# Layer norm applies ahead of the last k norm, tile 1's statistics on ScalarE, and a split V matmul pair at the start

## The chip, the cores and the metric

The kernel runs on one core of a Trainium2 chip. The metric is device time in microseconds (us), the median of several executions. All ratios below are the mean time of one kernel's fast runs over the mean time of the other's fast runs in the same rounds on the same chip, so they are not quite the ratio of the medians quoted beside them. The profile is of one execution, and its span, first to last instruction, is about 1.7 us shorter than the device time.

## The reference, cut to what matters

```python
xn = layernorm(x)                        # x: 2048 x 448, 16 tiles of 128 rows
q, k, v = split_heads(xn @ wqkv)         # 16 heads of 28
phi(t) = concat(softmax(t @ w_phi), softmax(-(t @ w_phi)))
attn = (phi(q) @ sum(phi(k)^T v)) / (phi(q) . sum(phi(k)) + 1e-6) @ wo
h    = gelu(layernorm(xn) @ w1)          # four quarters, shifted by 1, -1, 2, -2 rows
x1   = xn + shifted(h) @ w2
out  = x + attn + x1 + gelu(layernorm(x1) @ w3) @ w4
```

The first layer norm stands at the start of everything. The layer norm of `x1` ("LN2") needs `w2`'s output; the softmax of k ("k norm") is needed by the matmuls that sum `phi(k)^T v` ("kv").

## The kernel before

Every operation is recorded with what it reads and writes, and the waits between engines follow from that. The order on each engine is the order of recording. TensorE works mostly in pairs of 64-row matmuls, one on the lower and one on the upper half of its rows, and a product comes in two halves: in the second each row half goes to the other's output bank.

```python
def lap_pair(outs, lhs, rhs):
    ...
    return (lambda: row_pairs(side(0, LO, (0, 1, 2, 3)), side(1, HI, (0, 1, 2, 3)), True),
            lambda: row_pairs(side(1, LO, (0, 1, 3)), side(0, HI, (0, 2, 3))))

def ln1_two(i):                     # first layer norm, tiles 0..3
    for j in (i, i + 1):
        ln_stats(st, mv, xtok, j)                              # VectorE
        R.act(rs[:, j, 1:2], mv[:, j, 1:2], ACT.Sqrt, bias=epsb[:, 0:1])   # ScalarE
    for j in (i, i + 1):
        R.ew(dve, "reciprocal", rs[:, j, 0:1], rs[:, j, 1:2])
        ln1_apply(dve, j)

ln1_two(0)
spin(19, 256)                       # filler matmuls
play([(xn_T, 0, 0), (spin, 3, 256), (xn_T, 1, 1)])             # transposes and eviction
ln1_two(2)
...
play([(spin, 4, 256), V(0, 0), (xn_T, 2, 0), V(0, 1), (xn_T, 3, 1),
      (spin, 2, 256), V(2, 0), (v_out, 0, 2), (tables, "gelu_apprx_tanh_and_others"),
      WA(0, 0), (xn_T, 4, 1), V(2, 1), ...

def k_norm(i):
    ph = phik[:, i:i + 2, :, 0:DH].rearrange("p t g e -> p (t g) e")
    ...
    R.ew(dve, "tensor_reduce", k, ph, axis=AX.X, op=ALU.add)
    R.ew(dve, "reciprocal", rk, k)
    R.ew(pool, "tensor_tensor", ph, ph, rk..., op=ALU.mult)    # GpSimd, 3.2 us
...
play([(g_apply, 4, dve), (g_apply, 5, dve), G(4, 5), (ln_scale, mv2, rs2, 6, 2, 0),
      (g_apply, 6, dve), (g_apply, 7, dve), G(6, 7),
      a(0), (wl[11][0],), b(0), a(1), K(10, 11), b(1), K(12), a(2), K(13), b(2), a(3), K(14, 15), ...
```

`g_apply` is the apply of LN2, `G` the DMA that transposes its result into `gT`, `a` and `b` the two halves of a `w3` pair that reads `gT`, `K` the kv matmuls, `WA` the first matmuls of the gelu branch.

The softmax here doesn't subtract the row's maximum and nothing guards it: scores larger than these inputs give would overflow.

Of the kernel before, what the change touches and what calls it, by code (L numbers as in the profile page):

```python
# [5 lines left out]
ACT = mybir.ActivationFunctionType  # L6
ALU = mybir.AluOpType
AX = mybir.AxisListType
BF16 = mybir.dt.bfloat16
F32 = mybir.dt.float32  # L10

LN_EPS = 1e-5
# [208 lines left out]
def bass_parallel_sum__linear_kernel_hedgehog__mixer_s_mlp__prompt_kernel(  # L221
    nc, A_x, A_wqkv, A_w_phi, A_wo, B_x, B_w1, B_w2, B_w3, B_w4, out,
):
    _, S, D = A_x.shape
    H, DH = A_w_phi.shape[0], A_w_phi.shape[1]
# [10 lines left out]
    with es:  # L236
        R = Recorder(nc, es)
# [13 lines left out]
        def new(name, cols, dt=BF16):  # L251
            return view(region(name, cols * DTB[dt]), cols, dt)
# [6 lines left out]
        banks = [pairs[b // 2][:, 512 * (b % 2):512 * (b % 2) + 512] for b in range(8)]  # L259


        xtok = new("xtok", NT * D).rearrange("p (t d) -> p t d", t=NT)
        xn = new("xn", NT * 512).rearrange("p (t d) -> p t d", t=NT)
        xnT_r = region("xnT", KC * S * 2)
        xnT = view(xnT_r, KC * S).rearrange("p (c s) -> p c s", c=KC)
# [38 lines left out]
        ksum = new("ksum", 4 * 32, F32).rearrange("p (b c) -> p b c", b=4)  # L304
        rks = new("rks", 4 * 32, F32).rearrange("p (b c) -> p b c", b=4)
        mhalf = new("mhalf", 8, F32)
        epsb = new("epsb", 8, F32)

        h3T = view(phik_r, 2 * FC * 512).rearrange("p (b c f) -> p b c f", b=2, c=FC)
        oT = view(xnT_r, 2 * KC * 512).rearrange("p (b c s) -> p b c s", b=2, c=KC)  # L310
# [74 lines left out]
        def tables(name):  # L385
            R.op("ACT", lambda e: e.preload_act_table_set(name), [], [])

        tables("sqrt_and_others")
        R.ew(pool, "memset", ident[:, :], 0.0)
        R.op(pool, lambda e: e.affine_select(ident[:, :], ident[:, :], pattern=[[-1, 128]],  # L390
                                             compare_op=ALU.not_equal, fill=1.0, base=0, channel_multiplier=1),
# [4 lines left out]
        R.ew(pool, "memset", hD[:, :, 512:DW], 0.0)  # L396
        busy = gT[:, 0, 0, 0:256]
        R.ew(dve, "memset", busy, 1.0)
        R.ew(dve, "memset", epsb[:, :], LN_EPS)
        R.ew(dve, "memset", vp[:, :, DH + 1:HP], 0.0)  # L400
        R.ew(dve, "memset", vp[:, :, DH:DH + 1], 1.0)
        mb = maskb[0:CR, :].rearrange("p (h e) -> p h e", h=4)
# [33 lines left out]
        def ln_stats(stt, mvt, src, i):  # L436
            R.ew(dve, "bn_stats", stt[:, i, 0:6], src[:, i, 0:D])
            R.ew(dve, "bn_aggr", mvt[:, i, 0:2], stt[:, i, 0:6])
# [17 lines left out]
        def ln1_apply(eng, i):  # L456
            ln_apply(eng, halves(xn[:, i, :]), lap(xtok[:, i, :]), mv, rs, i)
# [3 lines left out]
        def spin(n, cols):  # L461
            for _ in range(n):
                R.mm(banks[7][:, 0:cols], busy[:, 0:128], busy[:, 0:cols], True, True)
# [51 lines left out]
        def row_pairs(first, second, start=False, cols=1):  # L515
            for s, (p, q) in enumerate(zip(first, second)):
                for out, lhs, rhs in (p, q) if cols == 1 else (*p, *q):
                    R.mm(out, lhs, rhs, start and s == 0, False)

        def lap_pair(outs, lhs, rhs):  # L520
            def side(k, rows, kcs):
                return [(outs[k], lhs(k, kc, *rows), rhs(k, kc, *rows)) for kc in kcs]
            return (lambda: row_pairs(side(0, LO, (0, 1, 2, 3)), side(1, HI, (0, 1, 2, 3)), True),
                    lambda: row_pairs(side(1, LO, (0, 1, 3)), side(0, HI, (0, 2, 3))))
# [9 lines left out]
                            lambda k, kc, lo, hi: xnT[lo:hi, kc, 512 * g:512 * g + 512])  # L534

        def v_pair(i, b):
            return lap_pair([banks[2 * b + k][:, 0:D] for k in range(2)],
                            lambda k, kc, lo, hi: xnT[lo:hi, kc, 128 * (i + k):128 * (i + k) + 128],
                            lambda k, kc, lo, hi: wv[lo:hi, kc, :])

        def v_out(i, b, eng="ACT"):
            vd = vaug[:, i:i + 2, :].rearrange("p t (h e) -> p t h e", e=HP)[:, :, :, 0:DH]
# [80 lines left out]
            e = (eq_lo if g < 2 else eq_hi)[:, c:c + 2, s, 512 * (g % 2):512 * (g % 2) + 512]  # L623
            R.act(e, two(2 * b), ACT.Exp, scale=1.0 - 2.0 * s)

        def k_norm(i):
            ph = phik[:, i:i + 2, :, 0:DH].rearrange("p t g e -> p (t g) e")
            r = 2 * (i // 2 % 2)
            k, rk = (t[:, r:r + 2, :].rearrange("p b c -> p (b c)") for t in (ksum, rks))
            R.ew(dve, "tensor_reduce", k, ph, axis=AX.X, op=ALU.add)  # L630
            R.ew(dve, "reciprocal", rk, k)
            R.ew(pool, "tensor_tensor", ph, ph, rk.unsqueeze(2).to_broadcast([128, 4 * H, DH]), op=ALU.mult)

        def kv_tile(i):
            def side(k, rows):
# [32 lines left out]
        def g_apply(i, eng="POOL"):  # L668
            ln_apply(eng, halves(g_tok[:, i % 4, :]), lap(xn[:, i, :]), mv2, rs2, i)

        def g_T(i):
            j = 128 * (i % 4)
            R.dma_t(gT[:, (i // 4) % 2, :, j:j + 128], g_tok[:, i % 4, :])
# [106 lines left out]
        def play(fs):  # L780
            for f in fs:
                f[0](*f[1:])

        def ln1_two(i):
            for j in (i, i + 1):
                ln_stats(st, mv, xtok, j)
                R.act(rs[:, j, 1:2], mv[:, j, 1:2], ACT.Sqrt, bias=epsb[:, 0:1])
            for j in (i, i + 1):
                R.ew(dve, "reciprocal", rs[:, j, 0:1], rs[:, j, 1:2])
                ln1_apply(dve, j)  # L790

        ln1_two(0)
        spin(19, 256)
        play([(xn_T, 0, 0), (spin, 3, 256), (xn_T, 1, 1)])
        ln1_two(2)
        for i in range(4, 10):
            ln1_stats(i, 1, 0)
            if i > 4:
# [24 lines left out]
        def V(i, k):  # L823
            return (vps[i][k],)

        def WA(g, k):
            return (was[g][k],)
# [7 lines left out]
        def FO(t, m, k):  # L835
            return (fps[t, m][k],)

        play([(spin, 4, 256), V(0, 0), (xn_T, 2, 0), V(0, 1), (xn_T, 3, 1),
              (spin, 2, 256), V(2, 0), (v_out, 0, 2), (tables, "gelu_apprx_tanh_and_others"), WA(0, 0), (xn_T, 4, 1),
              V(2, 1), (v_out, 2, 3), (xn_T, 5, 2), WA(0, 1), WC(0, 0), (xn_T, 6, 3), WC(0, 1), (wc_out, 0, 1),  # L840
              V(4, 0), (xn_T, 7, 3), (wa_out, 0, 0), V(4, 1), (v_out, 4, 2), V(6, 0),
              WC(1, 0), V(6, 1), (v_out, 6, 3), WA(1, 0), (xn_T, 8, 2, 2), WC(1, 1), (wc_out, 1, 1), WA(1, 1), (wa_out, 1, 0),
# [20 lines left out]
        for ps in range(8):  # L863
            k, q = k_pair(2 * ps, 1), q_pair(ps // 2, 2 * (ps % 2), 0)
            w = (w2_pair if ps else v_pair)(side[ps], 2)
            if not ps:
                play([(k[0],), (w[0],), (k[1],), (k_exp, 0, 1, 0), (k_exp, 0, 1, 1), (q[0],), (w[1],), (v_out, 12, 2, "DVE"),
                      V(14, 0), (q[1],), (q_exp, 0, 0, 0), (q_exp, 0, 0, 1), V(14, 1), (v_out, 14, 3), (k_norm, 0)])
                continue
            k[0]()  # L870
            if ps > 2:
                kv_tile(2 * ps - 6)
                kv_tile(2 * ps - 5)
            w[0]()
            k[1]()
            for s in range(2):
                k_exp(2 * ps, 1, s)
            q[0]()
            w[1]()
            w2_out(side[ps], 2)  # L880
            q[1]()
            for s in range(2):
                q_exp(2 * ps, 0, s)
            if ps in (3, 5):
                ln_scale(mv2, rs2, ps - 3, 2, 2)
                for i in (ps - 3, ps - 2):
                    g_apply(i)
                    g_T(i)
            if ps == 7:
                ln_scale(mv2, rs2, 4, 2, 0)  # L890
            k_norm(2 * ps)
            for i in ((), (0,), (1,), (2,), (3,), (4,), (5,), (6, 7))[ps]:
                ln_stats(st2, mv2, xn, i)

# [23 lines left out]
        def G(*t):  # L918
            return (lambda: [g_T(i) for i in t],)
# [4 lines left out]
        def A(*t):  # L924
            return (lambda: [g_apply(i) for i in t],)

        play([
            (g_apply, 4, dve), (g_apply, 5, dve), G(4, 5), (ln_scale, mv2, rs2, 6, 2, 0), (g_apply, 6, dve), (g_apply, 7, dve), G(6, 7),
            a(0), (wl[11][0],), b(0), a(1), K(10, 11), b(1), K(12), a(2), K(13), b(2), a(3), K(14, 15), b(3), (kv_copy,),
            a(4), (w2_last, 11), b(4), a(5), (kv_blocks,), b(5),  # L930
            a(6), N(0), (w2_norm, 8), b(6), a(7), f(1, 0), b(7), N(1), (w2_norm, 10), A(8, 9, 10, 11),
# [53 lines left out]
```

## Time and profile before

| | before |
|---|---|
| device time, median of 3 (range) | 174.38 us (174.19 to 174.67) |
| span of the profiled execution | 172.7 us |
| TensorE busy | 168.5 us, 98% of the span |
| first transposes start | 5.43 us |
| first k matmul starts | 30.58 us |
| first `w4` matmul starts | 82.56 us |

The lines of the profile before are in the prediction.

### The profile page before, as it was taken

What the parts mean: (1) busy time and instruction counts of PE and PEld (TensorE: products, weight loads), DVE (VectorE), ACT (ScalarE), POOL (GpSimd) and SP (SyncE); (2) the same over time, 40 slices, a digit from 0 to 9 for tenths busy, and PEclk for the clock granted to TensorE, in tenths of its full rate; (3) what the DMA queues carried; (4) which work ended last, traced back from release to release, by engine and by line L of the source; (5) the groups of instructions that cost most, each with busy time, mean ns of one, the idle gap of its engine ahead of it and who ended that gap; (6) DMA issues with size and microseconds to landing.
All of it is one profiled execution on the core that took longest, in us unless ns stands there. A gap on an engine that the chain in (4) does not pass through costs nothing.

```text
span 172.7 us, 5218 instructions
## 1 busy us (share of the span) xinstructions
PE 168.5 (98%) x2272; PEld 91.3 (53%) x2272; DVE 114.2 (66%) x263; ACT 84.4 (49%) x99; POOL 88.8 (51%) x123
## 2 busy tenths in 40 slices
PE   7899999999999999999999999999999999999994
PEld 5465576544555554554555555545545555545553
DVE  4999976277999999976587962445417425474621
ACT  3599874988778877947225322224204222224000
POOL 3066570015789999930639389440720714522740
DMA  5994461239942011034102933034411310312331
GB/s 169 339 195 82 81 167 42 57 45 363 382 154 46 16 34 30 4 36 89 33 1 61 96 61 83 4 87 93 93 30 55 85 33 4 84 30 34 84 86 54
DMA packets 32679, 15.21 MB, mean 88 GB/s; under 512 B 23952, under 2 KB 32016, under 8 KB 32656
## 3 DMA queue, kind: packets, MB, share of 16 engines
q1 hardware_dynamic: 32096, 14.51, 36.3%
q8 instruction: 18, 0.29, 0.8%
q10 hardware_dynamic: 560, 0.37, 0.7%
q14 instruction: 5, 0.04, 0.1%
HBM read 7.14 MB, written 1.84 MB: 52 GB/s over the span
## 4 chain that ended last, share of the span: by engine, by line
PE 95%; DVE 2%; issue 1%; ACT 0%
PE bank L200 94%; PE bank L204 1%; DVE vaug L212 1%; DVE st L212 1%; ACT xnT L208 0%; DVE xn L212 0%; DVE mv L212 0%; DVE gT L212 0%; DVE rs L212 0%; DVE epsb L212 0%
## 5 line engine op out<-in xcount | busy, mean ns | idle before, releaser
L208 ACT ACTIVATE phik<-bank 128x1024 bf16<-128x1024 f32 (+1 forms) x44 | 42.3, 984 | 60.5 <-PE bank L200 60.5
L200 PE MATMUL bank<-gT,w 64*128 64x512 bf16 x392 | 50.2, 377 | 0.1
L212 DVE TENSOR_TENSOR vaug<-bank,vaug 128x464 f32<-128x464 f32 (+3 forms) x65 | 32.7, 512 | 22.5 <-PE bank L200 20.9
L200 PE MATMUL bank<-w,phik 64*128 64x448 bf16 (+3 forms) x434 | 45.2, 343 | 0.0
L212 POOL TENSOR_TENSOR xnT<-vaug 128x196 bf16<-128x196 f32 (+1 forms) x32 | 18.1, 587 | 46.6 <-DVE vaug L212 46.6
L200 PEld LDWEIGHTS bank<-w,phik 64*128 64x128 bf16 (+1 forms) x434 | 22.9, 94 | 20.3 <-issue 0.4
L212 POOL TENSOR_TENSOR phik<-phik,rks 128x1792 bf16<-128x1792 bf16 x8 | 25.6, 3216 | 10.4 <-DVE rks L212 10.3
L200 PEld LDWEIGHTS bank<-gT,w 64*128 64x128 bf16 x392 | 17.8, 94 | 17.6 <-issue 0.6
L212 POOL TENSOR_TENSOR vaug<-xn,xtok 128x448 f32<-128x448 bf16 x16 | 16.2, 1032 | 0.2 <-DVE vaug L212 0.2
L212 DVE RECIPROCAL vaug<-bank 128x16 f32<-128x16 f32 x16 | 4.1, 257 | 18.3 <-PE bank L200 18.3
L212 DVE TENSOR_REDUCE ksum<-phik 128x64 f32<-128x1792 bf16 x8 | 16.1, 2011 | 0.0
L200 PE MATMUL bank<-xnT,wpq 64*128 64x512 bf16 x112 | 14.7, 376 | 0.0
L200 PE MATMUL bank<-wv,xnT 64*128 64x448 bf16 x112 | 13.9, 351 | 0.1
L200 PE MATMUL bank<-wo,xnT 64*128 64x448 bf16 (+3 forms) x110 | 13.6, 343 | 0.0
L200 PE MATMUL bank<-xnT,w 64*128 64x512 bf16 (+2 forms) x168 | 13.4, 306 | 0.0
L200 PE MATMUL bank<-w,hT 64*128 64x448 bf16 x112 | 13.2, 349 | 0.0
L200 PE MATMUL bank<-wpk,xnT 64*128 64x448 bf16 x112 | 13.2, 349 | 0.0
L212 POOL TENSOR_TENSOR rs<-mv,mhalf 128x1 f32<-128x1 f32 (+2 forms) x16 | 10.8, 676 | 1.3
L212 DVE TENSOR_TENSOR xn<-bank,xn 128x512 bf16<-128x512 f32 (+1 forms) x16 | 9.2, 620 | 3.1 <-PE bank L200 3.1
L212 DVE BATCH_NORM_STATS2 st<-xtok 128x6 f32<-128x448 bf16 x16 | 9.8, 612 | 0.0
L212 POOL TENSOR_SCALAR mv<-mv 128x1 f32<-128x1 f32 (+2 forms) x16 | 3.8, 239 | 11.2 <-DVE mv L212 10.8
L212 POOL TENSOR_SCALAR g_tok<-xn,rs 128x512 bf16<-128x512 bf16 x12 | 9.1, 776 | 0.3
(67 smaller groups left out, 173.0 us busy)
## 6 DMA issues: line engine op xcount, KB each, us to landing
w<-in_B_w_dram SPq DMA_DIRECT2D x2, 896.0 KB, 5.9
out_dram<-vaug SPq DMA_DIRECT2D x15, 112.0 KB, 1.9
w<-in_B_w_dram SPq DMA_DIRECT2D x1, 1568.0 KB, 11.3
xtok<-in_A_x_dram SPq DMA_DIRECT2D x2, 448.0 KB, 6.6
xtok<-in_A_x_dram SPq DMA_DIRECT2D x2, 224.0 KB, 4.5
w<-in_B_w_dram SPq DMA_DIRECT2D x2, 224.0 KB, 4.6
wo<-in_A_wo_dram SPq DMA_DIRECT2D x2, 224.0 KB, 7.0
xtok<-in_A_x_dram SPq DMA_DIRECT2D x3, 112.0 KB, 2.7
```

The lines of the kernel that those rows point to most:

```text
L200: self.op("PE", lambda e: e.matmul(out, lhsT, rhs, start=start, stop=stop, skip_group_check=True), [out], [lhsT, rhs], tile=self._tile(lhsT))
L204: self.op("PE", lambda e: e.transpose(out, in_, ident), [out], [in_, ident], tile=self._tile(in_))
L208: self.op("ACT", lambda e: e.activation(out, in_, func, **kw), [out], [in_] + aps)
L212: self.op(eng, lambda e: getattr(e, name)(out, *args, **kw), [out], aps)
```

## The change

It has three intents. Applies 4 and 5 of LN2 leave the queue behind the last k norm and go ahead of it, and the norm is made to wait for them. Tile 1's mean and mean square come from two summing activations on ScalarE, and all reciprocal roots from GpSimd's power, so that the square root table, and with it the second table load (1.28 us at 10.38 in the profile before), is gone. V pair 0 is split at its first step, to fit the later arrival of tile 1.

```diff
-        tables("sqrt_and_others")
+        tables("gelu_apprx_tanh_and_others")
@@ V pair: early, late and mid parts
+            def early():
+                row_pairs(side(0, LO, (0,)), side(1, HI, (0,)), True)
+                if i > 3:
+                    mid()
+            def mid():
+                row_pairs(side(0, LO, (1, 2, 3)), side(1, HI, (1, 2, 3)))
@@
-        def k_norm(i):
+        def k_norm(i, between=()):
             ...
             R.ew(dve, "reciprocal", rk, k)
-            R.ew(pool, "tensor_tensor", ph, ph, ...)
+            for j in between:
+                g_apply(j, dve)
+            R.op(pool, lambda e: e.tensor_tensor(ph, ph, rb, op=ALU.mult), [ph],
+                 [ph, rk, *(g_tok[:, j % 4, :] for j in between)])
+            for j in between:
+                g_T(j)
@@
-        ln1_two(0)
-        spin(19, 256)
-        play([(xn_T, 0, 0), (spin, 3, 256), (xn_T, 1, 1)])
-        ln1_two(2)
+        ln1_sum(1, ACT.Copy, 1.0 / D, mv[:, 1, 0:1], 14)
+        ln1_sum(1, ACT.Square, D ** -0.5, sq, 15)
+        ... stats 0, eps 0, variance of 1, stats 2, apply 0, eps 2, stats 3, apply 1, eps 3, applies 2 and 3
+        spin(18, 256)
+        play([(xn_T, 0, 0), (spin, 5, 256), (xn_T, 1, 1)])
@@
-        play([(spin, 4, 256), V(0, 0), (xn_T, 2, 0), V(0, 1), (xn_T, 3, 1),
-              (spin, 2, 256), V(2, 0), (v_out, 0, 2), (tables, ...), WA(0, 0), ...
+        play([(xn_T, 2, 0), V(0, 0), (xn_T, 3, 1), V(0, 2), V(0, 1),
+              V(2, 0), V(2, 2), (v_out, 0, 2), WA(0, 0), ...
@@
-            k_norm(2 * ps)
+            k_norm(2 * ps, (4, 5) if ps == 7 else ())
@@
-            (g_apply, 4, dve), (g_apply, 5, dve), G(4, 5), (ln_scale, mv2, rs2, 6, 2, 0), ...
+            (ln_scale, mv2, rs2, 6, 2, 0), (g_apply, 6, dve), ...
```

More of the change, by code (lines that the diff above doesn't have):

```diff
@@ L306, in bass_parallel_sum__linear_kernel_hedgehog__mixer_s_mlp__prompt_kernel @@
         mhalf = new("mhalf", 8, F32)
-        epsb = new("epsb", 8, F32)
         h3T = view(phik_r, 2 * FC * 512).rearrange("p (b c f) -> p b c f", b=2, c=FC)
@@ L398, in bass_parallel_sum__linear_kernel_hedgehog__mixer_s_mlp__prompt_kernel @@
         R.ew(dve, "memset", busy, 1.0)
-        R.ew(dve, "memset", epsb[:, :], LN_EPS)
         R.ew(dve, "memset", vp[:, :, DH + 1:HP], 0.0)
@@ L536, in v_pair, with side @@
         def v_pair(i, b):
-            return lap_pair([banks[2 * b + k][:, 0:D] for k in range(2)],
-                            lambda k, kc, lo, hi: xnT[lo:hi, kc, 128 * (i + k):128 * (i + k) + 128],
-                            lambda k, kc, lo, hi: wv[lo:hi, kc, :])
+            def side(k, rows, kcs):
+                lo, hi = rows
+                return [(banks[2 * b + k][:, 0:D], xnT[lo:hi, kc, 128 * (i + k):128 * (i + k) + 128], wv[lo:hi, kc, :])
+                        for kc in kcs]
+            def early():
[4 more added lines that the diff above has]
+                row_pairs(side(0, LO, (1, 2, 3)), side(1, HI, (1, 2, 3)))
+            return early, lambda: row_pairs(side(1, LO, (0, 1, 3)), side(0, HI, (0, 2, 3))), mid
         def v_out(i, b, eng="ACT"):
@@ L631, in k_norm @@
             R.ew(dve, "reciprocal", rk, k)
-            R.ew(pool, "tensor_tensor", ph, ph, rk.unsqueeze(2).to_broadcast([128, 4 * H, DH]), op=ALU.mult)
+            for j in between:
+                g_apply(j, dve)
+            rb = rk.unsqueeze(2).to_broadcast([128, 4 * H, DH])
+            R.op(pool, lambda e: e.tensor_tensor(ph, ph, rb, op=ALU.mult), [ph],
+                 [ph, rk, *(g_tok[:, j % 4, :] for j in between)])
+            for j in between:
+                g_T(j)
         def kv_tile(i):
@@ L782, in play, with ln1_pow, ln1_eps, ln1_sum @@
                 f[0](*f[1:])
-        def ln1_two(i):
-            for j in (i, i + 1):
-                ln_stats(st, mv, xtok, j)
-                R.act(rs[:, j, 1:2], mv[:, j, 1:2], ACT.Sqrt, bias=epsb[:, 0:1])
-            for j in (i, i + 1):
-                R.ew(dve, "reciprocal", rs[:, j, 0:1], rs[:, j, 1:2])
-                ln1_apply(dve, j)
-        ln1_two(0)
-        spin(19, 256)
-        play([(xn_T, 0, 0), (spin, 3, 256), (xn_T, 1, 1)])
-        ln1_two(2)
+        def ln1_pow(j, at):
+            R.ew(pool, "tensor_tensor", rs[:, j, 0:1], mv[:, j, at:at + 1], mhalf[:, 0:1], op=ALU.pow)
+        def ln1_eps(j):
+            R.ew(dve, "tensor_scalar", mv[:, j, 2:3], mv[:, j, 1:2], LN_EPS, 1.0, op0=ALU.add, op1=ALU.mult)
+            ln1_pow(j, 2)
+        def ln1_sum(j, func, scale, acc, junk):
+            out, in_ = xn[:, junk, 0:D], xtok[:, j, :]
+            R.op("ACT", lambda e: e.activation(out, in_, func, scale=scale, accum_out=acc), [out, acc], [in_])
+        sq = st2[:, 1, 0:1]
+        ln1_sum(1, ACT.Copy, 1.0 / D, mv[:, 1, 0:1], 14)
+        ln1_sum(1, ACT.Square, D ** -0.5, sq, 15)
+        ln_stats(st, mv, xtok, 0)
+        ln1_eps(0)
+        R.ew(dve, "tensor_scalar", mv[:, 1, 2:3], mv[:, 1, 0:1], mv[:, 1, 0:1], -LN_EPS, op0=ALU.mult, op1=ALU.add)
+        R.ew(pool, "tensor_tensor", mv[:, 1, 4:5], sq, mv[:, 1, 2:3], op=ALU.subtract)
+        ln1_pow(1, 4)
+        ln_stats(st, mv, xtok, 2)
+        ln1_apply(dve, 0)
+        ln1_eps(2)
+        ln_stats(st, mv, xtok, 3)
+        ln1_apply(dve, 1)
+        ln1_eps(3)
+        ln1_apply(dve, 2)
+        ln1_apply(dve, 3)
+        spin(18, 256)
+        play([(xn_T, 0, 0), (spin, 5, 256), (xn_T, 1, 1)])
         for i in range(4, 10):
@@ L836, in FO @@
             return (fps[t, m][k],)
-        play([(spin, 4, 256), V(0, 0), (xn_T, 2, 0), V(0, 1), (xn_T, 3, 1),
-              (spin, 2, 256), V(2, 0), (v_out, 0, 2), (tables, "gelu_apprx_tanh_and_others"), WA(0, 0), (xn_T, 4, 1),
+        play([(xn_T, 2, 0), V(0, 0), (xn_T, 3, 1), V(0, 2), V(0, 1),
+              V(2, 0), V(2, 2), (v_out, 0, 2), WA(0, 0), (xn_T, 4, 1),
               V(2, 1), (v_out, 2, 3), (xn_T, 5, 2), WA(0, 1), WC(0, 0), (xn_T, 6, 3), WC(0, 1), (wc_out, 0, 1),
@@ L927, in bass_parallel_sum__linear_kernel_hedgehog__mixer_s_mlp__prompt_kernel @@
         play([
-            (g_apply, 4, dve), (g_apply, 5, dve), G(4, 5), (ln_scale, mv2, rs2, 6, 2, 0), (g_apply, 6, dve), (g_apply, 7, dve), G(6, 7),
+            (ln_scale, mv2, rs2, 6, 2, 0), (g_apply, 6, dve), (g_apply, 7, dve), G(6, 7),
             a(0), (wl[11][0],), b(0), a(1), K(10, 11), b(1), K(12), a(2), K(13), b(2), a(3), K(14, 15), b(3), (kv_copy,),
```

## The prediction

> **What bounds the kernel now.** I read the busy table first, then the chain of work that ended last, then the timeline of the two stretches that the diff touches: 0 to 26 us and 66 to 90 us. From the page, the busy table and the chain:
>
> ```profile
> PE 168.5 (98%) x2272; PEld 91.3 (53%) x2272; DVE 114.2 (66%) x263; ACT 84.4 (49%) x99; POOL 88.8 (51%) x123
> ...
> PE 95%; DVE 2%; issue 1%; ACT 0%
> ```
>
> TensorE is the bound, and 95% of the chain lies on it. A matmul's busy time also covers waits inside it, so I measured the pitch instead. In the undisturbed stretches of the PE timeline 8 matmuls of 448 columns start 0.76 us apart (0.095 each) and 8 of 512 columns 0.86 (0.1075 each). Pitch times count over all shapes, without the 28 warm-up matmuls, gives about 163 us of the 172.7 us span. Of the other 9.7 us, 5.4 pass before the first transpose, some 2 after the last matmul (the final add and store), and about 2 are stalls and fillers in between. Nothing in the diff removes a real matmul, so only part of those 2 us, and the start, can be won. The start, from the timeline:
>
> ```profile
> 1.74 1.28 ACT L386 ACT_TABLE_LOAD   x1 [1.74 <-PEq L970]
> ...
> 3.30 0.63 DVE L212 BATCH_NORM_STATS2 st<-xtok 128x6 f32<-128x448 bf16 x1
> ...
> 4.96 0.41 DVE L212 TENSOR_SCALAR xn<-xtok,mv,rs 128x512 bf16<-128x512 bf16 x1
> ...
> 5.43 0.29 PE L204 MATMUL bank<-ident,xn 64*128 64x64 bf16 x8 [0.52 <-DVE xn L212]
> ...
> 7.97 0.41 DVE L212 TENSOR_SCALAR xn<-xtok,mv,rs 128x512 bf16<-128x512 bf16 x1
> ...
> 9.51 0.57 POOL L212 TENSOR_TENSOR rs<-mv,mhalf 128x1 f32<-128x1 f32 x1
> ...
> 9.60 0.49 PEld L200 LDWEIGHTS bank<-wv,xnT 64*128 64x128 bf16 x7 [0.34 <-ACT xnT L208]
> ...
> 10.19 1.21 PE L200 MATMUL bank<-xnT,w 64*128 64x512 bf16 x8
> ...
> 10.38 1.28 ACT L386 ACT_TABLE_LOAD   x1
> ...
> 13.19 0.20 PEld L204 LDWEIGHTS bank<-ident,xn 64*128 64x128 bf16 x8 [0.19 <-issue]
> ```
>
> The first transposes wait for the layer norm of tile 0 (DVE, end 5.37). The first matmuls of the gelu branch start at 10.19; that is my mark for the front. Behind it the second table load holds ScalarE until 11.66, its evictions queue, and the transpose of tile 6 (13.19) comes late because its bank is still being emptied. The stretch where the last k norm ends:
>
> ```profile
> 70.88 3.21 POOL L212 TENSOR_TENSOR phik<-phik,rks 128x1792 bf16<-128x1792 bf16 x1
> ...
> 72.14 2.42 DVE L212 TENSOR_SCALAR g_tok<-xn,mv,rs 128x512 bf16<-128x512 bf16 x2
> ...
> 74.26 5.96 SPq L215 DMA_TRANSPOSE gT<-g_tok  x4
> ...
> 74.52 0.71 PEld L200 LDWEIGHTS bank<-vaug,phik 64*128 64x128 bf16 x32
> ...
> 75.19 0.74 DVE L212 TENSOR_SCALAR g_tok<-xn,mv,rs 128x512 bf16<-128x512 bf16 x2 [0.63 <-POOL rs L212]
> ...
> 80.75 1.99 PE L200 MATMUL bank<-gT,w 64*128 64x512 bf16 x14
> ...
> 81.67 0.57 PEld L200 LDWEIGHTS bank<-gT,w 64*128 64x128 bf16 x8 [0.59 <-issue]
> ```
>
> Two applies took 2.42 us where the next two took 0.74: they ended when GpSimd's norm ended (74.09). So the four transposing DMAs started at 74.26; by the DMA view the last was issued at 79.0 and landed 2.5 us later, at 81.5, and the weight loads that need it sat idle until 81.67. The run of 14 there took 1.99 us, elsewhere 1.69: a stall of 0.3 us.
>
> [...] an apply took 2.09 us at most, and 0.41 without the norm beside it. [...] the four applies at 21.21 took 1.57 us in all, back to back, though a power of 0.61 us ran beside them. [...] The trace has 1.28 us for the load and 0.60 for 512 elements[...]; whether an accumulated sum costs more this trace does not show. [...] (19 fillers took 3.65 us, 0.19 each, later ones 0.11)[...].
>
> **The change, part by part.**
>
> Part 1, start. Landings by the DMA view: tile 0 at 0.81+2.5 = 3.3, tile 1 at 0.81+2.7 = 3.5, tile 2 at 1.26+2.7 = 4.0, tile 3 at 1.70+3.4 = 5.1. ScalarE is free from 3.02, so its two sums run 3.5 to 4.1 and 4.1 to about 4.7[...]. On VectorE: statistics of tile 0 end at 4.15 as before; two one-column instructions of about 0.1 each until 4.3; statistics of tile 2 (0.63+0.18 with overlap) until 5.1; apply 0 from about 5.1, if the power is ready. GpSimd's power begins at 4.4 and ends at 4.97 (0.57, the row above). So apply 0 comes about 0.12 later than before (5.08 against 4.96) and the first transposes start at 5.55. Next: epsilon of tile 2, statistics of tile 3 to 6.3, apply 1 at 6.25 (its power, after ScalarE's square and a GpSimd subtraction of 0.2, is done near 5.85), epsilon of tile 3, apply 2 at 6.7, apply 3 at 7.4, when tile 3's power is done. Before: 5.48, 7.45 and 7.97. Tile 1 is later by 0.8, tiles 2 and 3 earlier by 0.75 and 0.5.
>
> On TensorE tile 1's lateness is what the split of V pair 0 is for: its first 2 matmuls sit ahead of tile 3's transposes, the other 12 behind. Tile 1 is evicted near 7.6 (0.28 for the transposes, 0.6 for the copy), the 2 matmuls run to 7.85, the transposes of tile 3 run 7.9 to 8.1, then 12 + 8 matmuls at 0.095 = 1.9 to 10.0. The eviction of tile 3 (8.7) is then no wait, which removes the 0.34 us idle at 9.60. The gelu branch starts at about 10.0 against 10.19: a gain of 0.2. VectorE reaches tile 4's statistics some 0.45 earlier too, so it does not take this back.
>
> Part 2, table load. It is gone from 10.38; the eviction of pair 2 ends near 12.6 instead of 13.07, and tile 6's transposes no longer wait. By pitch they were due at 13.08 and came at 13.22: a gain of 0.14. The rest of the 1.28 us lay beside TensorE's work and buys nothing. Sum of the front: -0.34.
>
> Part 3, the last k norm. Applies 4 and 5 now run 70.7 to 71.45 (0.74 for two) right behind the reciprocal, and the norm starts at 71.54 and ends at 71.54+3.21 = 74.75, 0.66 late. Tiles 4 and 5 are transposed from 71.2; tiles 6 and 7, whose scale waits on GpSimd behind the norm, are applied at 75.85 to 76.6, and their DMAs go at 76.3 and 77.55 and land by 80.1. They were due at 81.1, so the stall of 0.3 us goes. But the kv matmuls of tiles 14 and 15 need the norm: their weight loads began at 74.52 and can now begin at 74.8, and the first matmul comes at about 74.95 instead of 74.73. That gives back 0.22. Sum: -0.09.
>
> Total: -0.34 - 0.09 = -0.43, from 174.38 to about 173.95 us.
>
> **The rivals.**
>
> A: the small GpSimd powers and VectorE's applies exclude each other at the start. For it: [...]one-column GpSimd multiplications that took 0.34 beside an apply instead of 0.19. Against: the four undelayed applies. Then apply 0 would wait for the subtraction, apply 1 for tile 2's power (to 6.85), and apply 3 would end near 8.7; the gelu branch would start near 10.8. The front would lose 0.6 instead of gaining 0.2, and the time would be 174.7 to 174.8.
>
> B: the delayed norm costs more than the landing saved. If the kv wait were the whole 0.66, the last part would lose 0.36 and the time would be 174.4. Against it: the norm ended 0.43 before those loads, so only the overlap beyond that shows.
>
> C: ScalarE's sums are dear. If one takes 0.85[...], VectorE's second one-column instruction waits for the first sum and tile 2's statistics move by some 0.15; tile 1's power moves by 0.6 but has slack of 0.4. Time 174.1 to 174.2.
>
> D: the front gains more, because VectorE ran without a break from 8 to 25 us and everything behind it moves by its 0.5 us and not by TensorE's. Against: after 16 us the idle before weight loads is mostly for evictions of the work just done. Time 173.7.
>
> **Range and chances.** The centre leans a little to D over A: 173.9. A at its full size is 174.75, which I give 10%; B and C fall inside. At the low side all of the 1 us of fillers and stalls in the front would have to vanish. The three runs before spread over 0.48 us, so the range is 173.2 to 174.6. A change of 2% is 3.5 us, more than the 2 us of stalls between first and last matmul, so faster by 2% gets 1%; slower by 2% [...]1%; within 2% gets 98%.
>
> **What would show each step.** Right: the first transposes at 5.5 to 5.7; tile 3's apply at 7.4 to 7.5; the gelu branch at 10.0; a transpose of tile 6 with no idle before it; the k norm starting at 71.5 less the shift of the front; two applies before it in 0.74; weight loads for the kv of tile 14 that wait about 0.3 on GpSimd; 14 gT matmuls in 1.69 instead of 1.99. Wrong: applies over 0.6 us beside GpSimd's powers (A), an idle of over 0.5 before the kv loads (B), sums over 0.8 us (C), a gelu branch later than 10.3, or a shift at 14 us that is gone by 32 us because some other wait took it.

The sum came to -0.20 for the gelu branch, -0.14 for the table load and -0.09 for the last part, -0.43 us in all. The duration of ScalarE's sums, 3.5 to 4.1 and 4.1 to 4.7, is an estimate from the 0.60 us that 512 elements took. Rival A had a second ground: the two applies that took 2.42 us at 72.14. That a matmul's busy time covers waits shows in the 14 `gT` matmuls, 1.99 us with a stall and 1.69 without. "Warm-up matmuls" are the fillers.

## The result

The changed kernel took 174.14 us (median of 6, 173.82 to 174.64), the kernel before 174.55 us in 6 runs (174.19 to 174.79). The ratio is 0.9982, with a 95% interval of 0.9962 to 1.0002: the same within 2%. The changed kernel is 0.41 us faster by the medians and 0.31 us by the means, and the interval just includes no difference.

The profiled execution was the slowest of the six. Its span is longer than before (172.9 against 172.7 us), so it has to be read with care. From its page, the span, the busy line of TensorE with the others, and the chain by engine:

```profile
span 172.9 us, 5209 instructions
...
PE 168.5 (97%) x2267; PEld 90.1 (52%) x2267; DVE 112.1 (65%) x260; ACT 83.2 (48%) x98; POOL 91.2 (53%) x128
...
PE 94%; DMA 3%; DVE 1%; SPq 0%; ACT 0%; issue 0%
```

The busy line hardly differs. The chain has a new member, a DMA with 3%, which before had no place in it. The timeline of the start shows which; in each row stand the start, the duration, the engine, the operation, and in brackets the idle time ahead of it with what ended it:

```profile
3.59 0.58 ACT L807 ACTIVATE xn<-xtok 128x448 bf16<-128x448 bf16 x1 [0.58 <-DMA xtok<-in_A_x_dram]
...
4.07 0.19 ACT L807 ACTIVATION_READ_ACCUMULATOR xn<-xtok 128x1 f32 x1
...
5.23 0.38 DVE L212 TENSOR_SCALAR xn<-xtok,mv,rs 128x512 bf16<-128x512 bf16 x1
...
5.67 0.39 PE L204 MATMUL bank<-ident,xn 64*128 64x64 bf16 x8 [0.39 <-DVE mv L212]
...
6.11 0.63 DVE L212 BATCH_NORM_STATS2 st<-xtok 128x6 f32<-128x448 bf16 x1 [0.43 <-DMA xtok<-in_A_x_dram]
...
7.23 0.41 DVE L212 TENSOR_SCALAR xn<-xtok,mv,rs 128x512 bf16<-128x512 bf16 x1
...
8.07 0.41 DVE L212 TENSOR_SCALAR xn<-xtok,mv,rs 128x512 bf16<-128x512 bf16 x1 [0.44 <-POOL rs L212]
...
9.46 1.06 PEld L200 LDWEIGHTS bank<-wv,xnT 64*128 64x128 bf16 x14 [0.51 <-PE bank L200]
...
10.80 1.03 PE L200 MATMUL bank<-xnT,w 64*128 64x512 bf16 x8
...
13.59 0.20 PEld L204 LDWEIGHTS bank<-ident,xn 64*128 64x128 bf16 x8 [0.15 <-DVE mv L212]
```

ScalarE's sums are there (0.58 us, and a separate read of the sum of 0.19). But the statistics of tile 3 at 6.11 waited for their DMA, which landed 4.4 us after its issue in this execution; in the profile before it was 3.4. So apply 2 came at 7.23, apply 3 at 8.07, and the gelu branch at 10.80, later than the 10.19 of before. At the first k matmul this execution is 0.37 us behind (30.95 against 30.58).

The same stretch of the timeline at the last k norm:

```profile
71.14 0.74 DVE L212 TENSOR_SCALAR g_tok<-xn,mv,rs 128x512 bf16<-128x512 bf16 x2
...
71.96 3.21 POOL L643 TENSOR_TENSOR phik<-phik,rks 128x1792 bf16<-128x1792 bf16 x1 [0.85 <-DVE g_tok L212]
...
75.22 0.51 PEld L200 LDWEIGHTS bank<-vaug,phik 64*128 64x128 bf16 x32 [0.46 <-POOL phik L643]
...
76.27 0.73 DVE L212 TENSOR_SCALAR g_tok<-xn,mv,rs 128x512 bf16<-128x512 bf16 x2 [2.91 <-POOL rs L212]
...
81.26 1.68 PE L200 MATMUL bank<-gT,w 64*128 64x512 bf16 x14
...
82.57 2.58 PEld L200 LDWEIGHTS bank<-w,phik 64*128 64x128 bf16 x28
```

The two applies take 0.74 us where they took 2.42, and the norm starts behind them. The kv weight loads now wait for it (0.46 us idle at 75.22). The 14 `gT` matmuls take 1.68 us; the 1.99 of before and the idle ahead of their second part are gone. From the first k matmul to the first `w4` matmul this takes 51.83 us instead of 51.98: a gain of 0.15.

### The profile page after: what moved, and what is told of

It is laid out like the page before. It is cut to its first block, busy times and chain, and to the rows that moved or that the text cites. A ratio compares the mean times of both kernels' runs of the same rounds, so it can differ in the third digit from the quotient of the medians.

```text
span 172.9 us, 5209 instructions
## 1 busy us (share of the span) xinstructions
PE 168.5 (97%) x2267; PEld 90.1 (52%) x2267; DVE 112.1 (65%) x260; ACT 83.2 (48%) x98; POOL 91.2 (53%) x128
## 4 chain that ended last, share of the span: by engine, by line
PE 94%; DMA 3%; DVE 1%; SPq 0%; ACT 0%; issue 0%
PE bank L200 93%; DMA xtok<-in_A_x_dram 3%; PE bank L204 1%; SPq L218 0%; DVE st L212 0%; ACT xnT L208 0%; DVE xn L212 0%; DVE vaug L212 0%; DVE mv L212 0%
## 5 line engine op out<-in xcount | busy, mean ns | idle before, releaser
L212 POOL TENSOR_TENSOR rs<-mv,mhalf 128x1 f32<-128x1 f32 (+2 forms) x20 | 13.2, 662 | 4.1 <-DVE mv L212 2.7
L212 DVE BATCH_NORM_STATS2 st<-xtok 128x6 f32<-128x448 bf16 x15 | 9.2, 617 | 0.4 <-DMA xtok<-in_A_x_dram 0.4
L212 DVE BATCH_NORM_STATS2 st<-xn 128x6 f32<-128x448 bf16 x16 | 9.3, 580 | 0.0
```

Of the source, the lines that this page charges most:

```text
L212: self.op(eng, lambda e: getattr(e, name)(out, *args, **kw), [out], aps)
```

## The experiments

All kernels ran five rounds beside the kernel before. All gave the reference's result, except one. Its output is wrong, which doesn't matter for the time. The intervals of most ratios are about 0.17% wide to either side (0.3 us), so effects of 0.1 us have to be read from the profiles. Each profile is a single execution, so where several kernels share a stretch, I give the spread between them.

### The changed kernel again, and its two parts alone

`again` is the changed kernel without an edit. `tail_only` is the kernel before with the last k norm's part alone, `front_only` the changed kernel with that part taken back:

```diff
# front_only, against the changed kernel
-            k_norm(2 * ps, (4, 5) if ps == 7 else ())
+            k_norm(2 * ps)
-            (ln_scale, mv2, rs2, 6, 2, 0), (g_apply, 6, dve), ...
+            (g_apply, 4, dve), (g_apply, 5, dve), G(4, 5), (ln_scale, mv2, rs2, 6, 2, 0), ...
```

> The changed kernel once more, unchanged, to see whether the late landing of x tile 3 in its first profile (4.4 us after its issue, where the kernel before had 3.4) is chance. Theory (chance of one execution): the landing comes back to about 3.4 us, the 0.43 us idle of VectorE before the statistics of tile 3 goes, and the gelu branch starts near 10.2 instead of 10.80; time 0.2 to 0.3% below the kernel before. Rival (the change itself makes it late): landing again at 4.2 or more, gelu branch at 10.7 or later, time within 0.2%. In both the stall of the tensor engine between the two halves of V pair 0, back to back now, stays at 0.2 to 0.3 us.

> The kernel before with the last k norm part alone. Theory: the wait of the kv weight loads on the norm costs 0.13 to 0.2 us, the landing of the transposed tiles gains 0.3, so the kernel is 0.1 to 0.2 us (0.06 to 0.12%) faster than the kernel before. Rival (the late norm costs as much as it saves): ratio 1.000 or above, a kv stall of 0.3 us or more.

> The changed kernel with the last k norm as it was. Theory: the front gives the larger part of the 0.4 us, so 0.2 to 0.3 us (0.12 to 0.17%) faster than the kernel before when tile 3 lands after about 3.4 us. Rival (the front is no gain at all, as the first profile of the changed kernel has it, 0.37 us behind at 32 us): 1.000 or slower. The stall of 0.3 us before the second tile group of gT must be back in its profile.

| kernel | median us | ratio to before (95%) | tile 3: issue to landing | first k matmul | from there to first `w4` |
|---|---|---|---|---|---|
| before | 174.47 | 1 | 3.4 | 30.58 | 51.98 |
| changed, first profile | 174.14 (other rounds) | 0.9982 | 4.4 | 30.95 | 51.83 |
| `again` | 174.17 | 0.9979 (0.9963 to 0.9995) | 3.2 | 30.28 | 51.87 |
| `tail_only` | 174.41 | 0.9999 (0.9981 to 1.0018) | 3.6 | 31.20 | 51.87 |
| `front_only` | 174.27 | 0.9984 (0.9969 to 1.0000) | 3.6 | 30.32 | 51.97 |

The late tile was chance of one execution, as the first theory had it. The timeline of `again` at the start, statistics of tile 3 first:

```profile
5.45 0.62 DVE L212 BATCH_NORM_STATS2 st<-xtok 128x6 f32<-128x448 bf16 x1
...
5.53 0.29 PE L204 MATMUL bank<-ident,xn 64*128 64x64 bf16 x8 [0.48 <-DVE mv L212]
...
7.41 0.41 DVE L212 TENSOR_SCALAR xn<-xtok,mv,rs 128x512 bf16<-128x512 bf16 x1 [0.44 <-POOL rs L212]
...
8.80 1.06 PEld L200 LDWEIGHTS bank<-wv,xnT 64*128 64x128 bf16 x14 [0.50 <-PE bank L200]
...
10.14 1.03 PE L200 MATMUL bank<-xnT,w 64*128 64x512 bf16 x8
```

No wait ahead of the statistics now; apply 3 is at 7.41 and the gelu branch at 10.14. The parts add up in these traces. The front is worth 0.26 to 0.30 us (30.28 and 30.32 against 30.58), the last part 0.11 to 0.15 (51.83 to 51.87 against 51.98). In `front_only`, where the last part is undone, its stall is back, in the first row (14 matmuls in 1.98 us):

```profile
80.49 1.98 PE L200 MATMUL bank<-gT,w 64*128 64x512 bf16 x14
82.29 2.05 PE L200 MATMUL bank<-w,phik 64*128 64x448 bf16 x19
```

The whole profile of `again` is 0.4 us shorter than that of before (172.3 against 172.7), and 0.30 + 0.11 is 0.41. `tail_only`'s ratio does not resolve its 0.11 us; its expectation of at least 0.1 us holds in the trace only.

A third profile with the old last part, that of `one_table` below, has a smaller stall:

```profile
80.85 1.88 PE L200 MATMUL bank<-gT,w 64*128 64x512 bf16 x14
```

It takes 51.87 us for the stretch, where the other two take 51.98 and 51.97; its first k matmul comes at 30.68. With the new last part all seven profiles lie between 51.83 and 51.87 us. So the stall is there in all three profiles with the old part that ran at full rate, and in none with the new one, but what its removal is worth in time varies between nothing and 0.15 us.

### An unplanned difference: when TensorE gets to its full rate

`tail_only` has the same start as the kernel before, and yet it reached its first k matmul 0.62 us later. Here is the TensorE timeline of the start for the kernel before, ...

```profile
1.25 3.65 PE L200 MATMUL bank<-gT 128*128 128x256 bf16 x19 [1.25 <-DVE gT L212]
...
5.65 0.50 PE L200 MATMUL bank<-gT 128*128 128x256 bf16 x3
6.08 0.29 PE L204 MATMUL bank<-ident,xn 64*128 64x64 bf16 x8
...
6.85 0.96 PE L200 MATMUL bank<-wv,xnT 64*128 64x448 bf16 x7
```

... and for `tail_only`:

```profile
1.26 4.23 PE L200 MATMUL bank<-gT 128*128 128x256 bf16 x19 [1.26 <-DVE gT L212]
...
5.86 0.82 PE L200 MATMUL bank<-gT 128*128 128x256 bf16 x3
6.62 0.39 PE L204 MATMUL bank<-ident,xn 64*128 64x64 bf16 x8
...
7.49 0.36 PE L200 MATMUL bank<-wv,xnT 64*128 64x448 bf16 x1
```

Three fillers take 0.82 us instead of 0.50 and eight transposes 0.39 instead of 0.29: TensorE was still at its slow rate near 6.7 us, whereas before it had left it by 4.5. (Here the "slow rate" and the "full rate" are no more than these durations: a filler takes 421 ns at the one and 273 at the other. The granted clock of the profile reads 1.00 in both stretches, so it doesn't show this.) The same fillers also delay tile 1's transposes, and V pair 0 starts at 7.49 instead of 6.85. From there on the difference stays. In `front_only` it was slow as well (transposes of 0.39 us, five fillers in 0.97), yet it lost only 0.04 us against `again` at the first k matmul, because there the first V matmul waits for tile 1 until 7.15 in any case. The first profile of the changed kernel was slow too (0.39 us, five fillers in 1.11), but behind the fillers TensorE still sat idle for 0.20 us until tile 1 was ready, so there it was the late tile that set the time.

This also fits the scatter: of 48 runs of the kernel before, 17 took 174.6 us or more, of the changed kernel 1 of 12, and that one had its tile 3 late. That all 17 are of the slow rate is not shown: none of them was profiled, and the slow start of this code was seen only in `tail_only`'s run of 174.92 us.

To test it, I started the fillers later in both kernels (at 2.96 us in the profiles, instead of 1.25), and cut the first group to nine:

```diff
-        R.ew(dve, "memset", busy, 1.0)
+        R.ew(pool, "memset", busy, 1.0)      # behind GpSimd's other start work
-        spin(19, 256)                        # 18 in the changed kernel
+        spin(9, 256)
```

> The kernel before, with the fillers started some 1.5 us later (their data set by GpSimd behind its own start work) and 9 of them instead of 19[...]. Theory (the profiles so far differ in when a 256-column filler falls from 0.42 to 0.27 us; where it falls late, the kernel before starts V pair 0 at 7.49 instead of 6.85 and is 0.6 us behind from there on): most of its executions now fall on the late side, so its median is 0.3 to 0.9 us above the kernel before of the same rounds. Rival (the two groups of times of the kernel before, 174.2 to 174.5 and 174.8 to 175.0, have another cause): within 0.1 us of the kernel before, in two groups again.

> The changed kernel with the same late fillers (9 instead of 18). Theory: its V pair 0 waits for tile 1's late layer norm anyway (7.15), so a late full rate up to 7 us costs it little: 0 to 0.4 us over the changed kernel, and less than the same change costs the kernel before by at least 0.2 us. Rival: both lose the same.

`cold_before` took 176.12 us (ratio 1.0091, 1.0062 to 1.0120, of its fast runs), `cold_after` 176.10 (1.0078, 1.0040 to 1.0116). By the means of the fast runs they are 1.6 and 1.3 us above the kernel before; against the changed kernel, which did not run in these rounds, `cold_after` loses about 1.7 us (an estimate from the ratios 1.0078 and 0.9979 to 0.9982). Both expectations were missed. The first was too small (0.3 to 0.9 us), and for the second its rival holds: both lose about the same. In `cold_after`'s profile the first two matmuls of V pair 0 take 1.22 us, where they take 0.83 in `again`, so the edit delayed the full rate beyond the point that the changed kernel tolerates. Together, the start and the number of the fillers matter to the time; the edit does not tell them apart, and it does not show that the changed start is sturdier. What speaks for that are other profiles: with slow transposes (0.39 to 0.40 us) the new start reached the first k matmul at 30.32 us in `front_only` and at 30.40 in `unsplit` below, the old one at 31.20. One execution of `cold_before`, the profiled one, never got to full rate. From its page:

```profile
span 450.1 us, 5197 instructions
...
PE 444.9 (99%) x2262; PEld 182.6 (41%) x2262; DVE 115.4 (26%) x262; ACT 85.2 (19%) x99; POOL 89.1 (20%) x124
```

TensorE was busy through all of 450.1 us, and a pair matmul of 512 columns took 829 ns on average instead of 377. Its device time (451.91 us) agrees with this, while the granted clock of the profile reads 1.00 in all of it from 2.9 us to 450. It is a slow run.

### Does the late tile matter: its load moved ahead

```diff
-        load_x(3, 1)
+        load_x(3, 1, "ACT")      # ScalarE's queue, ahead of the first half of wv
```

> The changed kernel with x tile 3 issued from ScalarE's queue right behind tile 1, ahead of the first half of wv. Theory (VectorE waits for tile 3): it lands by 4.5, the idle of VectorE at 6.1 goes, apply 3 runs near 7.5 and the gelu branch starts at 10.2 to 10.3; 0.2 to 0.4 us faster than the changed kernel when that one lands tile 3 late, nothing when it does not. Rival (the evictions of ScalarE and the stall between the halves of V pair 0 set the front): tile 3 earlier, gelu branch unchanged within 0.1, same time as the changed kernel in the same rounds. The table load starts 0.45 later, at 2.2, which should not show, since tile 1 lands at 3.5.

It took 174.14 us, ratio 0.9982 (0.9964 to 1.0000), as `again` in the same rounds (0.9979). Tile 3 landed 2.9 us after its issue at 1.24 us, near 4.15, and the first k matmul came at 30.36. So the earlier load does nothing when the tile is not late, as expected, and no late case was caught. That the late tile cost 0.6 to 0.7 us rests on the two profiles that had one: the first of the changed kernel (4.4 us) and that of `one_ahead` below (4.3 us, gelu branch at 10.74).

### The split of V pair 0 undone

```diff
-  (xn_T, 2, 0), V(0, 0), (xn_T, 3, 1), V(0, 2), V(0, 1),
+  (xn_T, 2, 0), V(0, 0), V(0, 2), (xn_T, 3, 1), V(0, 1),
```

> The changed kernel with the split of V pair 0 undone: its whole first half ahead of tile 3's transposes, its second half behind them. Theory (back to back, the second half waits for the first to drain: weight loads idle 0.5 us at 8.8, some 0.25 us of stall): the transposes of tile 3 fill that wait, and the gelu branch starts 0.1 to 0.2 us earlier than the changed kernel's 10.14, near 10.0; 0.1 us faster. Rival (the split is needed, since tile 3 and its eviction come later without it): gelu branch at 10.2 or later, same time or slower.

It took 174.16 us (0.9989, 0.9977 to 1.0001). The gelu branch started at 10.09, a little earlier than 10.14, but the first fold matmul (`bank<-g_tok,hi`, which multiplies `w_phi` into the weights) came at 20.29 instead of 20.16, and the first k matmul at 30.40 instead of 30.28. My mark was at fault. The TensorE timeline shows it at tile 4's eight transposes. In the kernel before, and the same in `unsplit`, they come in two lots with a V matmul between them:

```profile
11.05 0.38 PE L204 MATMUL bank<-ident,xn 64*128 64x64 bf16 x5
11.24 0.36 PE L200 MATMUL bank<-wv,xnT 64*128 64x448 bf16 x1
11.27 0.25 PE L204 MATMUL bank<-ident,xn 64*128 64x64 bf16 x3
```

In `again` they come together:

```profile
11.00 0.28 PE L204 MATMUL bank<-ident,xn 64*128 64x64 bf16 x8
11.12 0.73 PE L200 MATMUL bank<-wv,xnT 64*128 64x448 bf16 x6
```

In the kernel before one of V pair 2's first two matmuls had started at 9.17, while the others waited until 9.60 for tile 3's eviction. My reading of this, not a measurement, is that the two row halves of TensorE are then out of step by one matmul, that the gelu branch's first matmul, 10.19, tells where the leading half is, and that the lagging one catches up at the transposes. Measured is this: from the gelu branch to the first fold matmul it takes 10.20 us in all four kernels with the two lots (`before`, `tail_only`, `unsplit`, and `one_table` below) and 10.02 or 10.03 in all the others that ran at full rate. So the split is worth 0.12 us against `again` (30.40 against 30.28). The profile of `unsplit` had a slow start, though (transposes of 0.40 us, five fillers in 0.97); against `front_only`, whose start was as slow, it is 0.08 (30.40 against 30.32). The split also leaves a wait of its own: the two halves of V pair 0 now follow each other directly, and the second's weight loads sat idle for 0.50 us, until 8.80, for the matmuls of the first. That row halves out of step are the cause is argued from these patterns, not tested by itself.

### The second table load alone

```diff
-        tables("sqrt_and_others")
+        tables("gelu_apprx_tanh_and_others")
-            R.act(rs[:, j, 1:2], mv[:, j, 1:2], ACT.Sqrt, bias=...)
+            R.act(rs[:, j, 1:2], mv[:, j, 1:2], ACT.Identity, bias=...)   # wrong result, same work
-              ... (v_out, 0, 2), (tables, "gelu_apprx_tanh_and_others"), WA(0, 0), ...
+              ... (v_out, 0, 2), WA(0, 0), ...
```

> The kernel before with one activation table from the start and Identity in place of Sqrt, so that the second load at 10.4 us goes; its results are wrong on purpose, the durations are the same. Theory (the table load is part of the front's gain, 0.14 us by the prediction): from the first matmuls of the gelu branch to the first fold matmul 10.0 to 10.1 us instead of 10.20, and 0.1 to 0.2 us faster than the kernel before. Rival (the load lies beside TensorE's work, and the gain between those marks comes from VectorE, which is half a microsecond earlier in the changed kernel): 10.2 as before, no difference of time.

It took 174.53 us, 1.0015 (0.9994 to 1.0036), and from the gelu branch to the first fold matmul 10.20 us, as before (10.30 to 20.50). The rival was right. The Identity activations took 0.28 to 0.29 us, as Sqrt's had (0.28 to 0.30). In the kernel before, removing the load gains nothing: it lay beside TensorE's work entirely. In the changed order, where VectorE is earlier, the load was not tested by itself.

### Tile 1's statistics back on VectorE

```diff
-        ln1_sum(1, ACT.Copy, ...); ln1_sum(1, ACT.Square, ...)
+        ln_stats(st, mv, xtok, 1)     # in turn: stats 1, apply 0, eps 1, stats 2, apply 1, ...
```

> The changed kernel with tile 1's statistics on VectorE (0.62 + 0.18 us) and its scale by GpSimd's power, as the other tiles'; no sums on ScalarE. Theory (VectorE's order of work sets the front): apply 1 at the same time as in the changed kernel (6.2 to 6.3), applies 2 and 3 later by 0.8 to 1.1 us, gelu branch near 10.8 instead of 10.14, 0.5 to 0.7 us slower than the changed kernel, so 0.1 to 0.4 us slower than the kernel before. Rival (TensorE's queue of V matmuls and their drain hide tile 3): gelu branch within 0.2 of 10.14.

Its median is 177.21 us, and the ratio of its three fast runs 1.0089 (1.0056 to 1.0122); the other three were slow. VectorE behaved as expected: apply 1 at 6.23, apply 2 at 7.37, apply 3 at 8.51. The gelu branch came at 12.80 though, 2 us later than expected, and the time is about 1.5 us above the kernel before instead of 0.1 to 0.4. Against `again`, the 20 V matmuls ahead of the gelu branch start 1.09 us later (9.10 against 8.01) and take 1.57 us longer (3.86 against 2.29). Three equal stretches of this fast run show a lower granted clock in the second (columns: stretch, its length, TensorE's busy time and instructions, granted clock as a share of full speed, share of the DMA engines, GB/s):

```profile
5.60:9.00 3.40, 1.73 (x33) 1.00 1.04 342
9.00:12.40 3.40, 3.34 (x26) 0.52 1.28 239
12.40:15.80 3.40, 3.40 (x60) 0.98 0.39 70
```

And of `again`:

```profile
5.60:9.00 3.40, 2.95 (x47) 1.00 1.08 357
9.00:12.40 3.40, 3.40 (x50) 1.00 1.28 218
```

With more gaps in the start TensorE was busy for only 1.73 of 3.40 us, and in the next stretch it was granted 0.52 of its clock. `one_ahead` below was busy for 2.45 us of the first stretch, and its mean granted clock was 1.000. Of the three fast runs of `tile1_dve` two had a mean granted clock of 0.99 (176.65 and 176.22 us), and the third, at 1.0, took 175.02. So it looks as if ScalarE's sums buy more than the time of VectorE's instructions: with them TensorE was busy for 2.95 of the 3.40 us and was granted 1.00 in the next stretch. That the gaps caused the lower clock is an inference; the gaps by themselves were not tested.

### The last k norm: one apply ahead of it, or no wait

```diff
# one_ahead, against the changed kernel
-            k_norm(2 * ps, (4, 5) if ps == 7 else ())
+            k_norm(2 * ps, (4,) if ps == 7 else ())
-            (ln_scale, mv2, rs2, 6, 2, 0), (g_apply, 6, dve), ...
+            (g_apply, 5, dve), G(5), (ln_scale, mv2, rs2, 6, 2, 0), (g_apply, 6, dve), ...
# no_wait, against the changed kernel
-                 [ph, rk, *(g_tok[:, j % 4, :] for j in between)])
+                 [ph, rk])
```

> The changed kernel with only tile 4's apply ahead of the last k norm. Theory: the norm starts 0.37 us earlier, ends before the kv weight loads want it, so the idle of 0.46 to 0.50 there goes (gain 0.13 to 0.17 us), and tiles 5 to 7 are still transposed in time, so no stall at the second group of gT: 0.1 to 0.2 us faster than the changed kernel, 51.7 us from the first k matmul to the first w4 matmul instead of 51.85. Rival (tile 5, blocked by the norm till its end, lands too late as in the kernel before): the stall of up to 0.3 us is back and the time is that of the changed kernel or above.

> The changed kernel without the last k norm's wait for the two applies; there is no data behind that wait, so no race. Theory[...]: the first apply is in by the time the norm is ready, [...]the second apply then takes over 2.5 us, the statistics of tiles 6 and 7 queue behind it, and the idle of the kv weight loads of about 0.48 us falls to 0.2 or none; 51.7 to 52.0 us from the first k matmul to the first w4 matmul, that is the changed kernel's 51.85 within 0.15. Rival[...]: the norm takes about 0.5 us longer or starts 0.7 later all the same, everything as in the changed kernel within 0.05.

`one_ahead` took 174.19 us; its ratio of 1.0004 (0.9971 to 1.0037) holds one run of 175.85 us at a granted clock of 0.99, and its other five were 173.74 to 174.50. From the timeline, the norm, the second apply and the kv weight loads:

```profile
71.59 3.21 POOL L643 TENSOR_TENSOR phik<-phik,rks 128x1792 bf16<-128x1792 bf16 x1 [0.53 <-DVE g_tok L212]
...
72.91 2.04 DVE L212 TENSOR_SCALAR g_tok<-xn,mv,rs 128x512 bf16<-128x512 bf16 x1
...
74.86 0.67 PEld L200 LDWEIGHTS bank<-vaug,phik 64*128 64x128 bf16 x32 [0.16 <-POOL phik L643]
```

Tile 5's apply is blocked until the norm is done, as expected, but that costs nothing, since tiles 5 to 7 still land in time. The idle of the kv loads is down from 0.46 to 0.16 us, and first k to first `w4` matmul takes 51.70 us, against 51.83 to 51.87 for the changed kernel.

`no_wait` took 174.58 us, 1.0010 (0.9998 to 1.0022). Its two applies, the norm and a late wait of TensorE's weight loads:

```profile
70.53 3.76 DVE L212 TENSOR_SCALAR g_tok<-xn,mv,rs 128x512 bf16<-128x512 bf16 x2
...
70.61 3.21 POOL L643 TENSOR_TENSOR phik<-phik,rks 128x1792 bf16<-128x1792 bf16 x1
...
79.02 0.11 PEld L200 LDWEIGHTS bank<-w 64*128 64x128 bf16 x4 [0.85 <-DVE w L212]
```

The view of the tile (`prof no_wait --tile g_tok`; shortest, median and longest of the four applies, in ns) tells which of the two waited:

```profile
L212 DVE TENSOR_SCALAR g_tok<-xn,mv,rs x4: 402/408/3437, 70.5 to 77.2; 128x512 bf16<-128x512 bf16 x4
```

The long one is the one that starts at 70.5, the first: it took 3.44 us and ended at 73.97, just behind the norm (73.82). The second then took 0.40. By the records the first apply had started 0.08 us ahead of the norm and was held up all the same. VectorE's statistics for tiles 6 and 7 queued behind the applies, then the copy of the kv sums behind their applies, and TensorE waited for those (0.85 us). First k to first `w4` matmul took 52.24 us, 0.26 more than before. My expectation was right that the norm blocks an apply, but wrong that the first one would be through by then; it set the total at 51.7 to 52.0 and missed the kv copy. So the odd wait in the change, with no data behind it, is what makes its last part a gain: without it, this part is a loss.

### A version with both corrections

`best` is the changed kernel with `one_ahead`'s and `early_x3`'s edits together.

> The changed kernel with only tile 4's apply ahead of the last k norm, and x tile 3 issued early from ScalarE's queue. Theory: both corrections add to what the change gained, so 51.7 us from the first k matmul to the first w4 matmul (the changed kernel 51.83 to 51.87), tile 3 landed before 4.5 us, the first k matmul near 30.35, span near 172.2, and 0.25 to 0.35% faster than the kernel before. Rival (the gain of 0.15 us in the last part is lost in the scatter of the start): ratio 0.998, as the changed kernel; only the trace then shows the part. If tile 3 lands late again although issued early, the theory of its queue is wrong.

It took 173.96 us (173.82 to 174.01, the narrowest range of all), before 174.61 in the same rounds: 0.9964 (0.9950 to 0.9977). The norm and the kv loads in its timeline:

```profile
70.97 3.21 POOL L643 TENSOR_TENSOR phik<-phik,rks 128x1792 bf16<-128x1792 bf16 x1 [0.53 <-DVE g_tok L212]
...
74.23 0.70 PEld L200 LDWEIGHTS bank<-vaug,phik 64*128 64x128 bf16 x32
```

No idle ahead of the kv loads at all. First k matmul at 30.29, 51.69 us from there to the first `w4` matmul, span 172.1. It beats the kernel before; against the changed kernel the trace shows 0.14 to 0.18 us in that stretch, while the ratio, with no run of the changed kernel in the same rounds, is only suggestive (0.9964 against 0.9979 and 0.9982).

## Why the prediction was right, and where not

The total came out close: -0.43 us predicted; -0.41 by the medians, -0.31 by the means of the same runs, and -0.41 by the traces of two executions that both reached full rate ahead of the first transposes (before and `again`), 0.30 of it in the front and 0.11 in the last part, where I had 0.34 and 0.09. That it is as close as this is partly luck. A term of 0.14 was not there and others filled its place (Part 2 below); both stretches differ by 0.1 us between profiles with the old order (30.58 and 30.68, 51.98 and 51.87); and three of the six runs before were among those of 174.6 us or more, which move the mean and the median. The absolute time, 174.14, lies 0.24 above my centre of 173.9, of which 0.17 is the kernel before having been 174.55 rather than 174.38 in these rounds.

- **Part 1, the order of the layer norm.** Right. First transposes at 5.53 (I had 5.55), apply 1 at 6.20 (6.25), apply 2 at 6.56 (6.7), apply 3 at 7.41 (7.4) in `again`. In the first profile tile 3's DMA upset it, a wait that I had read off (landing at 5.1, used at 5.5) but not named as a risk.
- **The gelu branch at 10.0.** It came at 10.14. "then 12 + 8 matmuls at 0.095" left out a term: V pair 0's second half waits for its first (weight loads idle for 0.50 us), where the kernel before had tile 2's transposes between the two. On the other side, by the reading under `unsplit`, my reference of 10.19 was the leading half of TensorE, and the lagging half was later. The two errors nearly cancel: at the first fold matmul the gain is 20.39 - 20.16 = 0.23, where I had 0.2 for this step.
- **Part 2, the table load, "a gain of 0.14".** Wrong. `one_table` shows none. The late transposes of tile 6 waited for an eviction that itself waited for TensorE; in the changed kernel their weight loads still sat idle for 0.15 us, where I had none (0.19 before). What filled its place in the sum: 0.03 more in the step above, and 0.07 between the first fold matmul and the first k matmul (10.12 us against 10.19). The cause of that stays open; it is neither the table load (10.18 in `one_table`) nor the split (10.11 in `unsplit`).
- **Part 3, the last k norm.** Right in mechanism and nearly in size: counted from the first k matmul, the norm starts 0.71 to 0.75 us later (I had 0.66), the kv matmuls are delayed by 0.13 to 0.17 us (I had 0.22), and the stall of 0.3 is gone. The weight loads ahead of the kv matmuls sat idle for longer than I had it, 0.46 to 0.50 us instead of 0.3, but the first matmul then followed them within 0.01 us instead of 0.2. The `tail_only` and `front_only` pair separates this part. One reading of mine was loose: not both applies ended with the norm in the kernel before, but only the first waited for it (2.09 us), and the second followed. I did not see that the second of the two applies was not needed ahead, nor what the explicit wait was for.
- **Rival A**, powers and applies excluding each other, did not happen: the applies beside powers of 0.56 to 0.65 us took 0.38 to 0.41 us. **B** was real, at a fifth to a quarter of its full 0.66. **C** was half real: a sum is 0.58 + 0.19 us, but the read of the first runs beside the next activation, which starts 0.57 us after the first, and it stayed within the slack. **D** is not needed.
- **One filler fewer.** The prediction took it to do no harm to TensorE's rate; that was not shown, and was too sure. The moment of full rate differs between two executions of the same start by some 2 us (by 4.5 us in the kernel before, after 6.7 in `tail_only`), and the one in which it was late paid 0.6 us.

## What to carry to other kernels

A norm of 3.21 us on GpSimd held up the applies on VectorE that met it: they took 2.04 (`one_ahead`), 2.09 (before) and 3.44 us (`no_wait`) instead of 0.41, the last although by the records it had started 0.08 us ahead. So place such an instruction by what VectorE has ready at that moment: put ahead of it only what frees something in time, and make the long one wait for it explicitly. In the start, two executions of the same fillers got to full rate some 2 us apart, and in `tile1_dve` 1.73 busy us of 3.40 were followed by 0.52 of the clock, so look at fillers' durations in several executions before explaining a few tenths. And a mark on TensorE's timeline can mislead: from the same mark to the same matmul it was 10.20 us in four kernels here and 10.02 or 10.03 in the others. Check that the same count of work lies between two marks in both kernels.
